# Reordering a fused retention and ELU-MLP kernel: an earlier k^T v' visit, a later first ELU, split input differences, another order of the last seven products

## The chip, the cores and the metric

The kernel runs on one core of a Trainium2 chip. The time is device time in microseconds (us), the median of several executions. Its engines are TensorE (PE for the matmuls, PEld for the loads of their weights), VectorE (DVE), ScalarE (ACT), GpSimd (POOL) and SyncE (SP), which issues the DMA transfers. Every engine works through its own instructions in program order and waits for the others by semaphores.

## The reference

A retention layer (batch 4, 8 heads, sequence 768, head width 64) is followed by a two-layer network with ELU on 3072 tokens, all in fp32:

```python
for t in range(S):
    state = gamma * state + k[:, :, t] (outer) v[:, :, t]
    y[:, :, t] = scale * q[:, :, t] @ state
x = y reshaped to (3072, 512)
h = x @ w_in                                  # (3072, 2048)
g = where(h > 0, h, exp(min(h, 0)) - 1)
out = g @ w_out                               # (3072, 512)
```

## The kernel before

The 3072 tokens go in six blocks (`tb` 0 to 5) of 512. Blocks 2 to 5 use Strassen's scheme (Winograd's form: seven products M1 to M7 instead of eight) once for the first layer in four "quadruples" `n` of the hidden units, and twice for parts of it and for the second layer. The second layer of a block is seven outer products `j`, taken in the order 1, 2, 6, 7, 5, 3, 4, and each of them is again seven small products `k` ("a seven"): four matmuls of 128 columns each. The small products accumulate in PSUM banks pa, pb, pd; M6 and M5 are added onto M1's bank pa, M3 onto the same bank after M5, and M4 onto M7's bank pd. Before a product is added onto a bank, what the bank holds must have been read.

The retention layer of the next block is spread over the present block as short visits: `scores` (step 0), `states` (step 1, the k^T v' products and the running sums of the state), and `outputs` (steps 2 to 4).

The ELU of a tile is two ScalarE passes (relu and exp) and a last VectorE operation, which is put off in a list `later`:

```python
def elu(g, h, depth=1, then=None):
    r = epool.tile([P, 512], FP32, name="r", tag="r", bufs=3)
    ...
    nc.scalar.activation(e, h, AF.Relu, scale=-1.0)       # L390
    nc.scalar.activation(e, e, AF.Exp, scale=-1.0)        # L391
    def last():
        nc.vector.scalar_tensor_tensor(g, e, -1.0, h, ALU.add, ALU.max)   # L394
        if then: then()
    while len(later) >= depth:
        later.pop(0)()
    later.append(last)
```

First layer of a block, and where the second begins (`sec`):

```python
def first_end(n, name, ps, x=None):
    g = gq[name][:, 2 * n : 2 * n + 2, :]
    nc.vector.tensor_tensor(out=g, in0=ps, in1=g if x is None else x, op=ALU.add)   # L748
    ...
    return lambda: elu(g, g, 3, combine if name == "C22" else None)   # combine: T3, T1 (L753)
...
for n in range(NQ):
    rest(n, 6)                       # M6 on TensorE
    u2[n] = kept(qa[n])              # copy out of PSUM on ScalarE
    if n == 0:
        for _ in tail: pass
    if end: end()
    pop()                            # one operation from `later`
    rest(n, 7)                       # M7
    m7 = kept(qd[n])
    pop(2)
    if n == 3:
        next(sec)                    # first two input differences of the second layer
    rest(n, 5)                       # M5
    end = first_end(n, "C12", qa[n])
    other = first_end(n, "C22", qa[n], m7)
    end()
    if n < 3:
        other()
        rest(n + 1, 1)               # M1 of the next quadruple
        first_end(n + 1, "C11", qa[n + 1])()
        rest(n, 4)                   # M4
        end = first_end(n, "C21", qd[n], u2[n])
        pop()
        if n == 0: bring(3)
        elif more: retention_step(tb + 1, n - 1)      # scores behind n = 1, states behind n = 2
for _ in range(2):
    next(sec)                        # two more differences; M1 and M2 of the first seven
other()
rest(3, 4)
end = first_end(3, "C21", qd[3], u2[3])
next(sec)                            # M6, M7 of the first seven
end()
flush()
for step, s in enumerate(sec):
    if step in (1, 3, 5):
        retention_step(tb + 1, 2 + step // 2)
    if s == ORDER2[-1]: break
tail = sec
```

One seven of the second layer, and the loop over the seven of them. `input_parts` makes the four differences of an input (L656), each on a tile of 128 x 512:

```python
def input_parts(j):
    ...
    for n, _ in enumerate(quarters_of_input(t, b11, b12, b21, b22)):   # 4 subtractions, L656
        if n == 1:
            yield                    # after the first two
    ts[j] = {1: b11, 2: b21, 3: b22, 4: t[:, 3], 5: t[:, 0], 6: t[:, 1], 7: t[:, 2]}

def inner(j):
    res = pool.tile([P, 2, 2, P], FP32, name="res", tag=tag)
    pa = bank("a")[:, 0, 0:P]
    product(j, 1, pa, True)          # L779
    m1 = copy(pa)                    # L787, ScalarE
    pb = bank("b")[:, 0, 0:P]
    product(j, 2, pb, True)
    add(res[:, 0, 0], pb, m1)        # L791, VectorE
    yield
    product(j, 6, pa, False)
    u2 = copy(pa)
    pd = bank("d")[:, 0, 0:P]
    product(j, 7, pd, True)
    yield
    product(j, 5, pa, False)
    add(res[:, 1, 1], pd, copy(pa))  # the seven's C22 sum
    yield
    product(j, 3, pa, False)
    nc.scalar.copy(res[:, 0, 1], pa) # L812
    yield
    product(j, 4, pd, False)
    add(res[:, 1, 0], pd, u2)
    sum_up(j, res.rearrange("p d t c -> p (d t c)"))   # adds of 128 x 512, stores (L820)
...
for at, j in enumerate(ORDER2):      # 1, 2, 6, 7, 5, 3, 4
    cur = inner(j)
    next(cur)                        # M1, M2
    if j == 1: yield "tail"
    for _ in before: pass            # M3, M4 and sum_up of the seven before
    if j == 2: flush(); next_input(2)     # four adds, L558
    if j == 5: next_input(6)              # four subtractions, L558
    if j == 1:
        next(cur)
        yield "elu"
        next(cur)
    if at + 1 < 7:
        inputs(ORDER2[at + 1])       # all four differences of the next input
    else:
        behind_last()
    if j != 1:
        next(cur)                    # M6, M7
        next(cur)                    # M5, C22's sum
    before = cur
    yield j
```

`sum_up(4)` adds the outer result of j = 7 and others (`kept2[7]`) to all four quarters at once and stores 256 KB. The weights of the small products are fetched one by one from DRAM into a ring of eleven tiles, in the order of their use (`to_fetch`).

Of the kernel before, what the change touches and what calls it, by code (L numbers as in the profile page):

```python
# [9 lines left out]
FP32 = mybir.dt.float32  # L10
# [7 lines left out]
def kernel(  # L18
# [32 lines left out]
    nc = tc.nc  # L51
# [414 lines left out]
    def bank(x):  # L466
        return ps_f.tile([P, 2, TH], FP32, name="p" + x, tag=x, bufs=2 if x == "a" else 1)
# [140 lines left out]
    for tb in range(2, NTB):  # L608
        for j in TWICE:
            m1, m2, *mine = [(tb, 0, j, k) for k in (1, 2, 6, 7, 5, 4, 3)]  # L610
            to_fetch += [m1] + before[:1] + [m2] + mine[:2] + before[1:] + mine[2:3]
            before = mine[3:]
        to_fetch, before = to_fetch + before, []
        for j in ORDER2:
            mine = [(tb, 1, j, k) for k in (1, 2, 6, 7, 5, 3, 4)]
            to_fetch += mine[:2] + before + mine[2:5]
            before = mine[5:]
        to_fetch, before = to_fetch + before, []
# [140 lines left out]
    def second_twice(tb, behind_last):  # L759
        quarter = lambda x, r, t: x[:, 4 * r : 4 * r + 4, P * t : P * t + P]  # L760
        ts, kept2 = {}, {}

        def inputs(j):
            for _ in input_parts(j):
                pass

        def input_parts(j):
            x, t = gq[INPUT2[j]], tpool.tile([P, 4, 4, P], FP32, name="ts", tag="ts")
            b11, b12, b21, b22 = (quarter(x, a, b) for a in range(2) for b in range(2))
            for n, _ in enumerate(quarters_of_input(t, b11, b12, b21, b22)):  # L770
# [4 lines that stand above are left out]
        def product(j, k, ps, begin):  # L775
            name, w = small_w.pop(0)
            assert name == (tb, 1, j, k)
            for f in range(4):
                nc.tensor.matmul(  # L779
                    ps, lhsT=w[:, f, :], rhs=ts[j][k][:, f, :], start=(begin and f == 0), stop=(f == 3),  # L780
                    skip_group_check=True,
                )
            fetch_small()

        def copy(ps):
            m = small.tile([P, P], FP32, name="ms", tag="ms")
            nc.scalar.copy(m, ps)  # L787
            return m

        def add(o, x, y):  # L790
            nc.vector.tensor_tensor(out=o, in0=x, in1=y, op=ALU.add)  # L791

        def inner(j):
            pool, tag = (mpool, "m") if j in (1, 6, 7, 5) else (hpool, "h")
# [3 lines that stand above are left out]
            m1 = copy(pa)  # L798
            pb = bank("b")[:, 0, 0:P]
            product(j, 2, pb, True)  # L800
            add(res[:, 0, 0], pb, m1)
# [7 lines that stand above are left out]
            add(res[:, 1, 1], pd, copy(pa))  # L809
# [5 lines that stand above are left out]
            add(res[:, 1, 0], pd, u2)  # L815
            sum_up(j, res.rearrange("p d t c -> p (d t c)"))

        def store(name, h):
            r, t = int(name[1]) - 1, int(name[2]) - 1
            nc.sync.dma_start(out[tb, r, t].rearrange("p d c -> p (d c)"), h)  # L820

        def sum_up(j, m):

            kept2[j] = m
            if j == 2:
                add(m, kept2[1], m)
                store("C11", m)
            elif j == 6:
                add(m, kept2[1], m)
            elif j == 5:  # L830
                add(m, kept2[6], m)
                h = hpool.tile([P, 512], FP32, name="h", tag="h")
                add(h, m, kept2[7])
                store("C22", h)
                add(kept2[7], kept2[6], kept2[7])
            elif j == 3:
                add(m, kept2[5], m)
                store("C12", m)
            elif j == 4:
                add(m, kept2[7], m)  # L840
                store("C21", m)

        for _ in input_parts(1):
            yield "input"
        yield "inputs"
        before = iter(())
        for at, j in enumerate(ORDER2):
            cur = inner(j)
            next(cur)
            if j == 1:  # L850
                yield "tail"
            for _ in before:
                pass
            if j == 2:
                flush()
                next_input(2)
            if j == 5:
                next_input(6)
            if j == 1:

                next(cur)
                yield "elu"
                next(cur)
            if at + 1 < 7:
                inputs(ORDER2[at + 1])
            else:
                behind_last()
            if j != 1:
                next(cur)
                next(cur)  # L870
            before = cur
            yield j
        for _ in before:
            yield "rest"
# [121 lines left out]
    for tb in range(2, NTB):  # L996
        more = tb + 1 < NTB
        qa, qd, u2, end = {}, {}, {}, None

        def rest(n, j):  # L1000
            if j == 1:
                qa[n] = ps_r.tile([P, 2, TH], FP32, name="qa", tag="r") if n == 0 else bank("a")
            if j == 7:
                qd[n] = ps_r.tile([P, 2, TH], FP32, name="qd", tag="r") if n == 3 else bank("bd"[n % 2])
            first_rest(n, j, qa[n] if j in (1, 6, 5) else qd[n])

        def bring(n):
            if more:
                load((tb + 1) * CPB + n)
                scale_v((tb + 1) * CPB + n)  # L1010

        def pop(count=1):
            for _ in range(count):
                if later:
                    later.pop(0)()

        bring(0)
        rest(0, 1)
        for _ in tail:
            pass  # L1020
        tail, parts = iter(()), combine_x_parts()
        for at, j in enumerate(TWICE):
            cur = first_twice(tb, j)

            next(cur)
            next(tail, None)
            next(parts, None)
            next(cur)
            for _ in tail:
                pass  # L1030
            next(parts, None)
            if at == 1:

                first_end(0, "C11", qa[0])()
                bring(1)
            next(cur)
            tail = cur
        next(tail)
        bring(2)

        sec = second_twice(tb, combine_x_twice if more else lambda: None)
        for n in range(NQ):

            rest(n, 6)
            u2[n] = kept(qa[n])
            if n == 0:
                for _ in tail:
                    pass
            if end:
                end()  # L1050
            pop()
            rest(n, 7)
            m7 = kept(qd[n])
            pop(2)
            if n == 3:
                next(sec)
            rest(n, 5)
            end = first_end(n, "C12", qa[n])
            other = first_end(n, "C22", qa[n], m7)
            end()  # L1060
            if n < 3:
                other()
                rest(n + 1, 1)
                first_end(n + 1, "C11", qa[n + 1])()
                rest(n, 4)
                end = first_end(n, "C21", qd[n], u2[n])
                pop()
                if n == 0:
                    bring(3)
                elif more:  # L1070
                    retention_step(tb + 1, n - 1)
        for _ in range(2):
            next(sec)
        other()
        rest(3, 4)
        end = first_end(3, "C21", qd[3], u2[3])
        next(sec)
# [6 lines that stand above are left out]
            if s == ORDER2[-1]:  # L1084
                break
        tail = sec
# [49 lines left out]
```

## Time and profile before

| | |
|---|---|
| time, median of 3 runs | 656.89 us (655.04 to 657.96) |
| span of the profiled execution | 655.2 us |
| granted TensorE clock, mean | 0.997 |
| busy, 500 to 550 us (second layer of block 4): PE, PEld, DVE, ACT | 49.28, 47.09, 40.05, 11.86 us |
| DMA | 134.16 MB, mean 205 GB/s |

A row of the timeline gives the start in us, the busy time in us, engine, line and operation, the tile written and the tiles read, the number of instructions merged into the row, and in brackets the idle time of the engine before it with what ended it. A matmul product of four weights is shown as eight records; records overlap, so the busy time of a row is longer than the distance to the next row of a full stream. Line 779 is a small product of the second layer, line 740 a product of the first layer, line 787 a copy out of PSUM, line 791 an add of the second layer, line 656 an input difference. The second layers begin at about 303, 405, 506 and 603 us in blocks 2, 3, 4 and 5.

### The profile page before, as it was taken

Reading aid. Unit: us, or ns where it says so; the run is one execution under the profiler, and the core shown is the slowest. Engines: PE = TensorE matmul, PEld = TensorE weight load, DVE = VectorE, ACT = ScalarE, POOL = GpSimd, SP = SyncE. Lnnn points to the kernel's source line nnn. Section 1 sums busy time; section 2 is a strip of 40 time slices with the busy share of each in tenths; the row PEclk is TensorE's granted clock in tenths of the full one; section 3 lists DMA queues with packets and bytes.
Section 4 is the critical chain, followed back from the end, with each engine's and each line's share of the span. In section 5 each row is a group of like instructions: output and inputs, shape, how many; then the busy total and the mean of one; then the engine's idle time right before and its main releaser. Section 6 shows DMA issues by size and latency. Waiting matters only on the chain.

```text
span 655.2 us, 15245 instructions
## 1 busy us (share of the span) xinstructions
PE 635.3 (97%) x6336; PEld 539.4 (82%) x6336; DVE 470.1 (72%) x825; ACT 237.6 (36%) x448; POOL 37.0 (6%) x36
## 2 busy tenths in 40 slices
PE   4899999999999999999999999999999999999997
PEld 4754444548888889988999988999988999988996
DVE  5688778658866736588867488867488958558964
ACT  7467641104441001555111465211454311366211
POOL 1000100000720000110000110000020000000000
PEclk9899999999999999999999999999999999999999
DMA  8648978446384766911788811788830688700793
GB/s 340 240 134 311 316 232 260 131 126 227 107 298 174 256 231 207 377 76 52 250 276 285 303 77 34 221 277 272 305 135 2 204 270 279 214 18 10 237 313 116
DMA packets 68724, 134.16 MB, mean 205 GB/s; under 512 B 5680, under 2 KB 23088, under 8 KB 66352
## 3 DMA queue, kind: packets, MB, share of 16 engines
q1 hardware_dynamic: 68656, 133.19, 60.9%
q8 instruction: 50, 0.82, 0.5%
q14 instruction: 18, 0.15, 0.1%
HBM read 109.05 MB, written 24.12 MB: 203 GB/s over the span
## 4 chain that ended last, share of the span: by engine, by line
PE 84%; DVE 12%; DMA 2%; issue 1%; SPq 0%; ACT 0%; DVEq 0%
PE pa L779 11%; PE pa L740 8%; PE pd L779 7%; PE hp L420 6%; PE pa L434 4%; PE pa L579 4%; PE pb L740 4%; PE pa L521 4%; PE pa L694 4%; DVE ts L656 3%; PE qa L740 3%; PE pb L779 3%; PE pd L579 2%; DVE gC L394 2%; PE pd L740 2%; PE pd L521 2%
## 5 line engine op out<-in xcount | busy, mean ns | idle before, releaser
L391 ACT ACTIVATE r<-r 128x512 f32<-128x512 f32 x96 | 60.5, 630 | 3.1
L787 ACT COPY ms<-pa 128x128 f32<-128x128 f32 x84 | 22.2, 265 | 107.0 <-PE pa L779 106.8
L779 PE MATMUL pd<-ts,wq 128*128 128x128 f32 x448 | 59.8, 276 | 1.1 <-DVE res L791 1.1
L779 PE MATMUL pa<-ts,wq 128*128 128x128 f32 x448 | 59.4, 275 | 1.3 <-ACT ms L787 1.3
L779 PEld LDWEIGHTS pa<-ts,wq 128*128 128x128 f32 x448 | 54.6, 192 | 2.3 <-ACT ms L787 2.1
L779 PEld LDWEIGHTS pd<-ts,wq 128*128 128x128 f32 x448 | 54.5, 192 | 2.2 <-DVE res L791 2.2
L390 ACT ACTIVATE r<-gC 128x512 f32<-128x512 f32 x64 | 40.0, 625 | 41.1 <-DVE gC L748 41.1
L779 PE MATMUL pa<-gC,wq 128*128 128x128 f32 x384 | 51.7, 278 | 0.4 <-ACT ms L787 0.4
L779 PEld LDWEIGHTS pa<-gC,wq 128*128 128x128 f32 x384 | 47.2, 192 | 1.5 <-ACT ms L787 0.5
L394 DVE SCALAR_TENSOR_TENSOR gC<-r,gC 128x512 f32<-128x512 f32 x64 | 46.7, 757 | 0.7 <-ACT r L391 0.7
L242 POOL TENSOR_TENSOR kvn<-kvn,vf 128x512 f32<-128x512 f32 x20 | 22.9, 1150 | 361.4 <-DMA kvn<-in_qkv_dram 201.6
L791 DVE TENSOR_TENSOR res<-pd,ms 128x128 f32<-128x128 f32 x56 | 16.1, 287 | 35.0 <-PE pd L779 32.6
L471 ACT COPY m<-pa 128x512 f32<-128x512 f32 x27 | 15.7, 581 | 66.1 <-PE pa L579 35.5
L656 DVE TENSOR_TENSOR ts<-gC,ts 128x512 f32<-128x512 f32 x48 | 33.0, 688 | 0.8
L656 DVE TENSOR_TENSOR ts<-gC 128x512 f32<-128x512 f32 x48 | 32.8, 684 | 0.0
L434 PE MATMUL pa<-gC,w_s 128*128 128x512 f32 x64 | 30.6, 600 | 0.0
L579 PE MATMUL pa<-gC,ws 128*128 128x256 f32 x128 | 28.6, 381 | 0.0
L579 PEld LDWEIGHTS pa<-gC,ws 128*128 128x128 f32 x128 | 24.1, 190 | 3.4
L779 PE MATMUL pb<-gC,wq 128*128 128x128 f32 x192 | 26.4, 277 | 0.3
L779 PEld LDWEIGHTS pb<-gC,wq 128*128 128x128 f32 x192 | 23.7, 192 | 1.0 <-DVE gC L394 1.0
L812 ACT COPY res<-pa 128x128 f32<-128x128 f32 x28 | 7.4, 265 | 46.1 <-PE pa L779 44.6
L748 DVE TENSOR_TENSOR gC<-qa,gC 128x512 f32<-128x512 f32 x8 | 5.5, 692 | 25.0 <-PE qa L740 18.3
(192 smaller groups left out, 1290.5 us busy)
## 6 DMA issues: line engine op xcount, KB each, us to landing
wq<-scratch_dram SPq DMA_DIRECT2D x228, 256.0 KB, 4.3
wraw<-in_w_dram SPq DMA_DIRECT2D x16, 1024.0 KB, 6.0
qk<-in_qkv_dram SPq DMA_DIRECT2D x24, 512.0 KB, 7.7
kvn<-in_qkv_dram SPq DMA_DIRECT2D x24, 512.0 KB, 8.2
scratch_dram<-so SPq DMA_DIRECT2D x22, 512.0 KB, 3.2
ws<-scratch_dram SPq DMA_DIRECT2D x7, 1024.0 KB, 8.0
scratch_dram<-w_s SPq DMA_DIRECT2D x8, 512.0 KB, 7.3
out_dram<-res SPq DMA_DIRECT2D x12, 256.0 KB, 4.6
```

What stands on the lines that cost most here:

```text
L242: eng.tensor_tensor(out=kv[:, 1], in0=kv[:, 1], in1=vf[:, i].unsqueeze(2).to_broadcast([C, H, D]), op=ALU.mult)
L390: nc.scalar.activation(e, h, AF.Relu, scale=-1.0)
L391: nc.scalar.activation(e, e, AF.Exp, scale=-1.0)
L394: nc.vector.scalar_tensor_tensor(g, e, -1.0, h, ALU.add, ALU.max)
L420: nc.tensor.matmul(hp, lhsT=w[n][:, fi, j // 2, j % 2, :], rhs=xb[:, j, :], start=(j == 0), stop=(j == 3))
L434: nc.tensor.matmul(ops[d], lhsT=wo[:, row, d * P : (d + 1) * P], rhs=g_plain[row * NF + f], start=(f == 0 and row == 0), stop=(f == NF - 1 ...
L521: nc.tensor.matmul(ps[:, fi, :], lhsT=w[:, fi, j2, :], rhs=x[:, j2, :], start=(begin and fi == 0 and j2 == 0), stop=(j2 == 1), skip_group_ ...
L579: nc.tensor.matmul(ps[:, d, :], lhsT=ws[:, 2 * d + f // 4, f % 4, :], rhs=gq[INPUT2[j]][:, f, :], start=(begin and f == 0 and d == 0), sto ...
L656: sub = lambda o, x, y: nc.vector.tensor_tensor(out=o, in0=x, in1=y, op=ALU.subtract)
L694: nc.tensor.matmul(ps[:, f, :], lhsT=lhs[f], rhs=xs[j][k], start=(begin and f == 0), stop=True, skip_group_check=True,)
L740: nc.tensor.matmul(ps[:, fi, :], lhsT=w[:, fi, j2, :], rhs=x[:, j2, :], start=(j in (1, 7) and fi == 0 and j2 == 0), stop=(j2 == 1), skip_ ...
L779: nc.tensor.matmul(ps, lhsT=w[:, f, :], rhs=ts[j][k][:, f, :], start=(begin and f == 0), stop=(f == 3), skip_group_check=True,)
```

## The change

Five moves, all of order:

1. In blocks 2 to 4 the `states` visit for the next block, which stood behind the third quadruple, now stands inside it, behind M7.
2. In the fourth quadruple of blocks 2 to 5, the ELU passes of C12 are issued behind M1 and M2 of the first seven instead of ahead of them; so the copy of M1 stands ahead of them in ScalarE's order.
3. During j = 2 and j = 5 of every block's second layer, only two of the next input's four differences are issued at the old place, the other two behind the seven's C22 sum.
4. In the last block the last seven (j = 4) takes M4 ahead of M3, on a bank of its own (pb), and the fetch order follows.
5. The last seven adds earlier results to each quarter by itself (where possible before the product) and stores its result in three transfers for four quarters of 64 KB: 64, 128 and 64 KB, instead of one of 256 KB.

It is for keeping TensorE from waiting at the start of the second layer, for reading bank pd in time, and for shortening what follows the last product.

```diff
@@ fetch order of the second layer
+            last = (4, 3) if j == 4 and tb == NTB - 1 else (3, 4)
+            mine = [(tb, 1, j, k) for k in (1, 2, 6, 7, 5) + last]
-            mine = [(tb, 1, j, k) for k in (1, 2, 6, 7, 5, 3, 4)]
@@ the last seven
+        def inner_end(j):
+            res = hpool.tile([P, 2, 2, P], FP32, name="res", tag="h")
+            to = out[tb, 1, 0].rearrange("p d (t c) -> p d t c", t=2)
+            k = kept2[7].rearrange("p (d t c) -> p d t c", d=2, t=2)
...         (M1, M2, M6 as in inner)
+            product(j, 7, pd, True)
+            m7 = copy(pd)
+            yield
+            add(u2, u2, k[:, 1, 0])
+            add(u2, pd, u2)
+            product(j, 5, pa, False)
+            add(res[:, 1, 1], pa, m7)
+            yield
+            add(res[:, 0, 0], res[:, 0, 0], k[:, 0, 0])
+            nc.sync.dma_start(to[:, 0, 0], res[:, 0, 0])
+            add(res[:, 1, 1], res[:, 1, 1], k[:, 1, 1])
+            pb = bank("b")[:, 0, 0:P]
+            product(j, 4, pb, True)
+            add(res[:, 1, 0], pb, u2)
+            nc.sync.dma_start(to[:, 1], res[:, 1])
+            product(j, 3, pa, False)
+            add(res[:, 0, 1], pa, k[:, 0, 1])
+            nc.sync.dma_start(to[:, 0, 1], res[:, 0, 1])
@@ loop over the sevens
-            cur = inner(j)
+            last = j == 4 and tb == NTB - 1
+            cur = (inner_end if last else inner)(j)
...
-            if at + 1 < 7:
-                inputs(ORDER2[at + 1])
+            parts = input_parts(ORDER2[at + 1]) if at + 1 < 7 else iter(())
+            if j in (2, 5):
+                next(parts)
             else:
+                for _ in parts:
+                    pass
+            if at == 6:
                 behind_last()
             if j != 1:
                 next(cur)
                 next(cur)
+            for _ in parts:
+                pass
@@ first layer
             pop(2)
+            if n == 2 and more:
+                retention_step(tb + 1, 1)
             if n == 3:
                 next(sec)
...
-            end()
             if n < 3:
+                end()
                 other()
...
-                elif more:
-                    retention_step(tb + 1, n - 1)
+                elif n == 1 and more:
+                    retention_step(tb + 1, 0)
         for _ in range(2):
             next(sec)
+        end()
         other()
```

More of the change, by code (lines that the diff above doesn't have):

```diff
@@ L816, in inner @@
             sum_up(j, res.rearrange("p d t c -> p (d t c)"))
+        def inner_end(j):
+            res = hpool.tile([P, 2, 2, P], FP32, name="res", tag="h")
+            to = out[tb, 1, 0].rearrange("p d (t c) -> p d t c", t=2)
+            k = kept2[7].rearrange("p (d t c) -> p d t c", d=2, t=2)
+            pa = bank("a")[:, 0, 0:P]
+            product(j, 1, pa, True)
+            m1 = copy(pa)
+            pb = bank("b")[:, 0, 0:P]
+            product(j, 2, pb, True)
+            add(res[:, 0, 0], pb, m1)
+            yield
+            product(j, 6, pa, False)
+            u2 = copy(pa)
+            pd = bank("d")[:, 0, 0:P]
+            product(j, 7, pd, True)
[5 more added lines that the diff above has]
+            add(res[:, 1, 1], pa, m7)
+            yield
+            add(res[:, 0, 0], res[:, 0, 0], k[:, 0, 0])
+            nc.sync.dma_start(to[:, 0, 0], res[:, 0, 0])
+            add(res[:, 1, 1], res[:, 1, 1], k[:, 1, 1])
+            pb = bank("b")[:, 0, 0:P]
+            product(j, 4, pb, True)
[4 more added lines that the diff above has]
+            nc.sync.dma_start(to[:, 0, 1], res[:, 0, 1])
         def store(name, h):
```

## The prediction

> **What bounds the kernel now.** I read the first part of the page, then the starts of all TensorE matmuls in order, then the timeline around each place where a start came late, and last the end of the program.
>
> ```profile
> span 655.2 us, 15245 instructions
> PE 635.3 (97%) x6336; PEld 539.4 (82%) x6336; DVE 470.1 (72%) x825; ACT 237.6 (36%) x448; POOL 37.0 (6%) x36
> ```
>
> TensorE sets the time. The change takes no matmul away, so it can only win idle TensorE time and time after the last matmul. The busy share hides short holes, because a matmul's shown duration overlaps the next one's start. I therefore measure from start to start. A product of four weights on 128 columns (line 779) takes 0.89 us to the next start, one on 256 columns (line 740) takes 1.73 us. What a product starts later than that is lost, and each restart after a wait costs 0.10 more (the first product after one takes 0.99).
>
> First kind of hole, timeline of block 2, where the second stage begins:
>
> ```profile
> 304.69 1.89 PE L740 MATMUL qd<-xt,w_b 128*128 128x256 f32 x8
> 305.94 0.63 ACT L390 ACTIVATE r<-gC 128x512 f32<-128x512 f32 x1 [3.96 <-DVE gC L748]
> 306.60 0.63 ACT L391 ACTIVATE r<-r 128x512 f32<-128x512 f32 x1
> 307.13 0.25 ACT L787 COPY ms<-pa 128x128 f32<-128x128 f32 x1
> 307.44 1.16 PE L779 MATMUL pa<-ts,wq 128*128 128x128 f32 x8 [0.85 <-ACT ms L787]
> ```
>
> M6 of the first seven could start at 304.69 + 1.73 = 306.42 and starts at 307.44. It adds onto bank pa, which must first be copied out. M1, whose sum the copy takes, started at 302.91 and was over at about 304.0, but the copy stands on ScalarE behind the two ELU passes of C12, and these wait for VectorE's C12 sum, done only at 305.9. VectorE is late because the k^T v' visit's adds stand just ahead. Loss 1.02 + 0.10 = 1.12 us. By the same sum, block 4 loses 0.63 + 0.10 = 0.73 (M6 at 509.94 for 509.31); blocks 3 and 5 lose nothing (408.44 and 606.54 are on time).
>
> Second kind, timeline of block 5, second seven (j = 2):
>
> ```profile
> 616.14 0.68 DVE L656 TENSOR_TENSOR ts<-gC 128x512 f32<-128x512 f32 x1
> 616.85 0.69 DVE L656 TENSOR_TENSOR ts<-gC,ts 128x512 f32<-128x512 f32 x1
> 617.54 1.06 PE L779 MATMUL pa<-gC,wq 128*128 128x128 f32 x8
> 618.07 0.69 DVE L656 TENSOR_TENSOR ts<-gC,ts 128x512 f32<-128x512 f32 x1
> 618.67 0.28 DVE L791 TENSOR_TENSOR res<-pd,ms 128x128 f32<-128x128 f32 x1
> 619.01 1.16 PE L779 MATMUL pd<-ts,wq 128*128 128x128 f32 x8 [0.41 <-DVE res L791]
> ```
>
> M4 adds onto pd, so C22's sum must have read pd. That sum had its operands at 616.2 (the copy of M5 ran from 615.96), but stands behind all four differences of the next input. Wanted 618.43, started 619.01: 0.58 + 0.10 = 0.68. The same hole is there for j = 5 in every block: 0.43, 0.43, 0.42 in blocks 2 to 4 (M4 at 342.10, 442.97, 544.62) and 0.43 in block 5 (638.19 for 637.87). For j = 3 in block 5 it is 0.17 + 0.10.
>
> Third, the end:
>
> ```profile
> 647.50 1.06 PE L779 MATMUL pa<-ts,wq 128*128 128x128 f32 x8
> 648.59 0.27 ACT L787 COPY ms<-pa 128x128 f32<-128x128 f32 x1 [1.52 <-PE pa L779]
> 648.91 1.16 PE L779 MATMUL pa<-gC,wq 128*128 128x128 f32 x8 [0.35 <-ACT ms L787]
> 649.91 1.06 PE L779 MATMUL pd<-ts,wq 128*128 128x128 f32 x8
> 651.00 0.29 DVE L791 TENSOR_TENSOR res<-pd,ms 128x128 f32<-128x128 f32 x1 [1.82 <-PE pd L779]
> 651.40 0.69 DVE L791 TENSOR_TENSOR res<-res 128x512 f32<-128x512 f32 x1
> ```
>
> M3 directly after M5 must wait for M5's copy (648.91 for 648.39: 0.52 + 0.10), and behind the last product come a small sum, a sum over all four quarters and a store of 256 KB, issued at 652.12, landed at 654.14, then 1.0 us of closing.
>
> **What the Trainium skill says.** "Perfetto Trace Analysis", Identifying the Most-Contended Engine, calls matmul busy time a poor measure of headroom and weight-load busy time a better one. Here they are 97% and 82%; the starts show why neither is enough, the holes being fractions of a microsecond. "VectorE: DVE Perf Modes", The TRN2 errata, gives an fp32 two-operand sum as (N+151)/0.96 ns: 691 ns at 512 and, worked out, 291 at 128. The trace agrees with 692 and 287 ns; so four quarter sums cost more in all than one large, and only the last one matters. "DMA: Bandwidth & Descriptors", Anatomy of one DMA, puts about 2.0 us of fixed cost on a transfer, most of it the write receipt. Here the whole 256 KB store took 2.02 us from issue to landing, data included: about 0.65 to the first packet, 1.0 of packets, 0.35 to the landing. The trace decides: about 1.0 us is fixed here, and the packets can be shortened.
>
> **The change, part by part.**
>
> *Visit earlier and C12's ELU behind the first copy (blocks 2 to 4; the second also 5).* No instruction is added. The visit (128 or 112 matmuls of 64 columns, then some seven VectorE adds of 424 ns) keeps its price on TensorE: it interrupts the stream once in either place. On VectorE in block 4 the adds run from 499.82 to 503.14, 3.3 us. In the quadruple before it VectorE idles 0.46 + 0.44 + 1.04 = 1.94 us waiting for products (block 2: 0.46 + 0.44 + 1.03). Put there, the adds use that idle time. My walk through the queue of block 4 delays the sums of the third quadruple by some 0.7 us and gets VectorE to the first input difference at about 505.3 instead of 506.40. The copy of M1, now ahead of the ELU, runs when M1 is done, at about 304.0 in block 2, 2.4 us before M6 wants it. Its other operand, the second difference (done at 305.3), is in time as well. So both holes close: **1.12 + 0.73 = 1.85 us**. Blocks 2 to 4 then look like block 5, which has no visit.
>
> A hole stays: M2 of the second seven waits for the last ELU of C21: 0.35, 0.32, 0.36 and 0.28 us in blocks 2 to 5, restart included. Block 5 has it without any visit, so I expect about 0.28 in each: **0.2 us** at most, counted as 0.1.
>
> *Half inputs.* Two of the four differences move behind C22's sum, which comes about 1.25 us earlier (two steps of 0.61 to 0.65). It must gain 0.58 at most, so the holes at j = 2 (block 5) and j = 5 (all) close: 0.68 + 0.43 + 0.43 + 0.42 + 0.43 = **2.39 us**. What moves back is wanted late: the third difference feeds M7 of the next seven, five products (4.5 us) after M5, the fourth M4. For j = 3 nothing changes and 0.27 stays.
>
> *The end.* With M4 (on its own bank pb) between M5 and M3, M4 starts at 648.39 and M3 at 649.28; C22's sum reads pa at 648.6 to 648.9, in time. **0.62 us**. The sums with earlier results move ahead of the last product: u2 takes its addend before M4 is over, two others are done meanwhile. Behind M3 stands one sum of 0.29 us, then its store: M3 ends at about 650.35, store issued at 650.70. Before, the end of M4 (650.97) to the issue took 1.15 us, now 0.35: **0.80 us**. The last store has 64 KB in 512-byte rows; such packets took 27 ns in this trace, the present ones of 2048 bytes 84 ns. Eight per engine: 8 x 57 ns = **0.46 us**. The other parts are issued 0.9 us and more ahead and should be written by then.
>
> Sum: 1.85 + 0.1 + 2.39 + 0.62 + 0.80 + 0.46 = 6.2 us, or 656.89 - 6.2 = 650.7. As one of five terms may come short I say 650.9.
>
> **Rivals.** *A new hole in the third quadruple.* The delayed C12 and C22 sums push three ELUs (ScalarE, 1.19 us each in a row) towards the copy of M6 of the fourth, for which M5 waits. In my walk that copy ends some 0.4 to 0.6 us before M5 wants it in blocks 2 and 4. Against it: the slack is positive. For it: it is small, and if the delay is one microsecond larger, each of three blocks loses up to 0.5. Then 652.2. *VectorE as the bound in the second stage.* It is 80% busy there (40.1 of 50 us from 500 to 550), and in block 5 runs without a break from 607.35 to 618.95. If each hole only moves to the next product that waits for VectorE, half of the 2.39 us is lost: 652. Against it: behind every C22 sum concerned VectorE had over 1 us of idle time waiting for products (1.05 before 620.20). *Weights arriving late.* A faster stream asks for its weights earlier, but the fetches run eleven tiles ahead (9.8 us of products) and land in 4.3 us; in blocks 2 to 5 no hole but one, at 258, waits for one. *The stores at the end in each other's way*: three issues of 0.34 us and an unfinished 128 KB ahead of the last 64 KB could take back 0.4 us.
>
> **Range and chances.** The gain can hardly exceed 7 us, as the holes touched sum to 4.9 and the end to 1.3; if two rivals come true it is 3.5. The times before spread over 2.9 us, so the median itself is uncertain by about one. From 649.0 to 653.5 covers both. Two per cent is 13.1 us, twice all that can be won; a loss of that size would need a new wait of several microseconds in every block. Faster 0.01, same 0.98, slower 0.01.
>
> **What would show it.** In the changed trace M6 of the first seven follows the qd product by 1.73 us in every block; M4 of j = 2 and j = 5 follows M3 by 0.89; the 0.27 at j = 3 and about 0.3 at M2 of the second seven stay; the last product has M3's form (pa), and the span's end comes some 3.0 us after it instead of 4.2. I'm wrong if M5 of the fourth quadruple waits for ScalarE, if M7 of j = 6 or 3 waits for VectorE, or if the span stays above 652.

## The result and the profile after

The changed kernel takes 651.8 us (median of 6 runs, 650.24 to 653.29) against 657.35 us for the kernel before in the same series: a ratio of 0.9918, 95% interval 0.9893 to 0.9943. Three later series gave 0.9898 (0.9868 to 0.9928), 0.9911 (0.9891 to 0.9931) and 0.9912 (0.9897 to 0.9927). That is a gain of 0.8 to 1.0 per cent, clear of the scatter in all four series and below two per cent. The prediction was 650.9 us.

Busy times from the page of the changed kernel, and its chain of work that ended last by engine:

```profile
PE 633.5 (97%) x6336; PEld 539.2 (83%) x6336; DVE 468.8 (72%) x829; ACT 237.7 (37%) x447; POOL 36.8 (6%) x36
...
PE 96%; DMA 1%; DVE 1%; issue 1%; SPq 0%; DVEq 0%
```

The same chain in the kernel before:

```profile
PE 84%; DVE 12%; DMA 2%; issue 1%; SPq 0%; ACT 0%; DVEq 0%
```

Busy shares have hardly moved. What moved is the chain: before, 84% of it lay on TensorE and 12% on VectorE; now 96% and 1%. The 12% is the work on VectorE through which the chain ran, not time lost: the whole gain is about 1%. What is left of waits for VectorE in blocks 2 to 5 is 0.28 us at M2 of each second seven and 0.27 at j = 3 in block 5, restarts included. Code lines are shifted by one and more against the kernel before (779 is now 780, 787 is 788, 791 is 792). The timelines show only the rows that the argument needs.

Timeline of block 2, where the second layer begins:

```profile
304.95 0.27 ACT L788 COPY ms<-pa 128x128 f32<-128x128 f32 x1 [2.03 <-PE pa L780]
305.39 0.63 ACT L390 ACTIVATE r<-gC 128x512 f32<-128x512 f32 x1 [0.17 <-DVE gC L749]
305.65 1.89 PE L741 MATMUL qd<-xt,w_b 128*128 128x256 f32 x8
307.38 1.05 PE L780 MATMUL pa<-ts,wq 128*128 128x128 f32 x8
```

M1's copy is made as soon as M1 is over, and M6 starts 1.73 us after the qd product: no loss (1.02 before).

Timeline of block 5, second seven (j = 2):

```profile
615.76 0.69 DVE L657 TENSOR_TENSOR ts<-gC,ts 128x512 f32<-128x512 f32 x1
616.37 0.28 DVE L792 TENSOR_TENSOR res<-pd,ms 128x128 f32<-128x128 f32 x1
616.45 1.06 PE L780 MATMUL pa<-gC,wq 128*128 128x128 f32 x8
616.57 0.68 DVE L657 TENSOR_TENSOR ts<-gC 128x512 f32<-128x512 f32 x1
617.34 1.06 PE L780 MATMUL pd<-ts,wq 128*128 128x128 f32 x8
```

C22's sum stands behind two differences instead of four, and M4 starts 0.89 us after M3.

Timeline of the end; the stores are on the SP queue:

```profile
645.30 1.06 PE L780 MATMUL pa<-ts,wq 128*128 128x128 f32 x8
646.19 1.06 PE L780 MATMUL pb<-ts,wq 128*128 128x128 f32 x8
647.09 1.06 PE L780 MATMUL pa<-gC,wq 128*128 128x128 f32 x8
647.29 0.29 DVE L792 TENSOR_TENSOR res<-pb,ms 128x128 f32<-128x128 f32 x1 [0.20 <-PE pb L780]
648.18 0.29 DVE L792 TENSOR_TENSOR res<-pa,res 128x128 f32<-128x128 f32 x1 [0.60 <-PE pa L780]
648.50 0.33 SPq L851 DMA_DIRECT2D out_dram<-res  x1
```

M5, M4 and M3 follow each other at 0.89 us. From the last product's end (648.14) to the store's issue are 0.36 us (1.15 before), from issue to landing 1.55 (2.02 before).

One hole is new. In this profile TensorE stands still in block 2, in the middle of a product:

```profile
332.51 0.82 PE L780 MATMUL pa<-gC,wq 128*128 128x128 f32 x5
...
334.33 0.60 PE L780 MATMUL pa<-gC,wq 128*128 128x128 f32 x3 [1.00 <-issue]
```

The sixth record was due at 333.16 and starts at 334.33: 1.17 us, and 0.10 of restart, with no instruction to wait for. It is followed up below.

A single span depends on this and on the first 45 us, so I compare the distances between the starts of successive blocks' first products, in us. Block 2 also has up to 0.5 us of waiting for weights at its start, different in each profile. A star marks profiles with the standstill (its size in brackets).

| kernel | block 2 | block 3 | block 4 | block 5 to end |
|---|---|---|---|---|
| before | 100.70 | 100.87 | 101.66 | 99.38 |
| changed, first profile | 99.90* (1.27) | 100.40 | 100.42 | 96.35 |
| changed, second profile | 99.06 | 100.41 | 100.42 | 96.35 |
| visit alone | 101.21* (1.82) | 100.82 | 100.84 | 99.35 |
| copy ahead of ELU alone | 101.17* (0.80) | 100.85 | 101.64 | 99.36 |
| half inputs alone | 99.81 | 100.44 | 101.22 | 98.26 |
| last seven alone | 100.60 | 100.86 | 101.64 | 97.44 |
| order of the last seven alone | 102.04* (1.54) | 100.87 | 101.66 | 98.59 |
| changed, copy behind ELU again | 98.84 | 100.41 | 100.42 | 96.35 |
| changed, two differences later | 99.49 | 100.86 | 100.87 | 96.53 |
| changed, one difference on GpSimd | 99.54 | 100.60 | 100.62 | 96.27 |
| changed, finer order | 98.34 | 100.12 | 100.13 | 95.80 |

### The profile page after: what moved, and what is told of

Same layout as the page of the kernel before. It is cut to its first block, busy times and chain, and to the rows that moved or that the text cites. A ratio compares the mean times of both kernels' runs of the same rounds, so it can differ in the third digit from the quotient of the medians.

```text
span 651.1 us, 15255 instructions
## 1 busy us (share of the span) xinstructions
PE 633.5 (97%) x6336; PEld 539.2 (83%) x6336; DVE 468.8 (72%) x829; ACT 237.7 (37%) x447; POOL 36.8 (6%) x36
## 4 chain that ended last, share of the span: by engine, by line
PE 96%; DMA 1%; DVE 1%; issue 1%; SPq 0%; DVEq 0%
PE pa L780 16%; PE pa L741 10%; PE pd L780 8%; PE hp L420 6%; PE pa L695 4%; PE pa L434 4%; PE pa L579 4%; PE pb L741 4%; PE pa L521 4%; PE pb L780 4%; PE qa L741 3%; PE pd L695 2%; PE pd L579 2%; PE qd L741 2%; PE pd L521 2%; PE pd L741 2%
## 5 line engine op out<-in xcount | busy, mean ns | idle before, releaser
L780 PE MATMUL pd<-ts,wq 128*128 128x128 f32 x440 | 58.2, 275 | 0.0
L394 DVE SCALAR_TENSOR_TENSOR gC<-r,gC 128x512 f32<-128x512 f32 x64 | 44.5, 727 | 0.7 <-ACT r L391 0.7
```

Of the source, the lines that this page charges most:

```text
L780: nc.tensor.matmul(ps, lhsT=w[:, f, :], rhs=ts[j][k][:, f, :], start=(begin and f == 0), stop=(f == 3), skip_group_check=True,)
```

## The experiments

**The four parts, one at a time.** Each is the kernel before with one part of the change.

*The visit alone:*

```diff
             pop(2)
+            if n == 2 and more:
+                retention_step(tb + 1, 1)
...
-                elif more:
-                    retention_step(tb + 1, n - 1)
+                elif n == 1 and more:
+                    retention_step(tb + 1, 0)
```

> The kernel before with the states visit alone moved behind M7 of the third quadruple. My theory: VectorE reaches C12's sum of the fourth quadruple about 1.1 us earlier, so the copy of M1, still behind C12's ELU passes, ends before M6 wants it; M6 of the first seven is on time in blocks 2 and 4: 1.12 + 0.73 = 1.85 us and about 0.1 at M2 of the second seven, block 2 shorter by 1.2, block 3 by 0.05, block 4 by 0.8, block 5 unchanged. Rival one: the copy must also get ahead of the ELU, then at least 0.3 us stays at M6 in block 2. Rival two: the visit's adds delay C12 and C22 of the third quadruple so that M5 of the fourth waits for ScalarE, 0.3 to 0.5 us in each of blocks 2 to 4.

Measured: ratio 0.9966 (0.9956 to 0.9976), 2.2 us. Block 2 without the standstill 99.4, block 4 shorter by 0.82, block 3 by 0.05, as my theory had it. In the kernel before, where M1 starts at 302.91, VectorE's first input difference of block 2 is this row:

```profile
303.89 0.69 DVE L656 TENSOR_TENSOR ts<-gC 128x512 f32<-128x512 f32 x1
```

Timeline of block 2 with the visit moved; the second row is M1:

```profile
303.92 0.68 DVE L656 TENSOR_TENSOR ts<-gC 128x512 f32<-128x512 f32 x1
304.44 1.05 PE L779 MATMUL pa<-gC,wq 128*128 128x128 f32 x8
...
305.97 0.63 ACT L390 ACTIVATE r<-gC 128x512 f32<-128x512 f32 x1 [2.47 <-DVE gC L748]
...
307.17 0.25 ACT L787 COPY ms<-pa 128x128 f32<-128x128 f32 x1
...
307.95 1.05 PE L779 MATMUL pa<-ts,wq 128*128 128x128 f32 x8
```

VectorE's date shows the cause. In the kernel before, its first input difference starts 0.98 us after M1 in block 2 and 0.60 after it in block 4, but 0.17 ahead in block 3 and 0.51 ahead in block 5, which has no visit. With the visit moved, it starts 0.51 to 0.52 us ahead of M1 in all four blocks. The copy still stands behind an ELU, but the ELU now starts early enough: copy over at 307.42, M6 at 307.95, 1.73 after the qd product (306.23). No wait at M5 of the fourth quadruple (rival two) is to be seen.

*The copy ahead of the ELU alone:*

```diff
-            end()
             if n < 3:
+                end()
                 other()
...
         for _ in range(2):
             next(sec)
+        end()
         other()
```

> The kernel before with C12's ELU passes of the fourth quadruple alone issued behind M1 and M2 of the first seven. My theory: M6 is on time everywhere (gain 1.85 us), but VectorE is as late as before, so C12's and C22's ELU passes end late and the copy of M6 behind them ends late: a new hole at M5 of the first seven, about 0.6 us in block 2 and 0.1 to 0.2 in block 4. Net gain about 1.0 us. Rival: this move alone closes everything, 1.85 us, and the visit's move brings nothing.

Measured: ratio 1.0002 (0.9990 to 1.0014), nothing. The rival fell, and of my theory only the hole at M5 came true (0.40 us for 0.6); the net gain did not. Timeline of block 2:

```profile
308.27 0.25 ACT L787 COPY ms<-pa 128x128 f32<-128x128 f32 x1
...
308.57 1.16 PE L779 MATMUL pa<-ts,wq 128*128 128x128 f32 x8 [0.24 <-ACT ms L787]
...
311.02 0.68 DVE L394 SCALAR_TENSOR_TENSOR gC<-r,gC 128x512 f32<-128x512 f32 x1
...
311.76 0.71 PE L779 MATMUL pb<-gC,wq 128*128 128x128 f32 x4 [0.69 <-DVE gC L394]
```

M6 is on time, but M5 now waits 0.40 and M2 of the second seven 0.86 (0.25 before), plus 0.10 each. Its input is C21's last ELU operation, which ends 7.05 us after the start of the qd product here (311.70 and 304.65) and 7.06 us after it in the kernel before (311.75 and 304.69): in both kernels VectorE works from 303.9 to that date without a break, so its queue alone sets it. The hole of 1.12 merely moved to the next products that depend on VectorE; in block 4 nearly all of it moved to M2 (0.85, 0.26 before).

*The half inputs alone:*

```diff
-            if at + 1 < 7:
-                inputs(ORDER2[at + 1])
+            parts = input_parts(ORDER2[at + 1]) if at + 1 < 7 else iter(())
+            if j in (2, 5):
+                next(parts)
...
+            for _ in parts:
+                pass
```

> The kernel before with the half inputs alone (j = 2 and j = 5). My theory: M4 of j = 2 in block 5 and of j = 5 in blocks 2 to 5 start 0.89 us after M3: gain 2.39 us, 0.43 in each of blocks 2 to 4 and 1.11 in block 5; the 0.27 at j = 3 in block 5 stays. Rival: VectorE is the bound there and half of it comes back at the next product that waits for it (M7 of j = 6 or j = 3, or M4 of j = 6): gain 1.2 us.

Measured: ratio 0.9958 (0.9946 to 0.9970), 2.8 us. Blocks 3 and 4 shorter by 0.43 and 0.44, block 5 by 1.12; the 0.27 at j = 3 stays. No hole comes back; the rival fell.

*The last seven alone* (`inner_end` and its fetch order), and *its order alone*, with one sum and one store as before:

```diff
+            m7 = copy(pd)
...
+            add(u2, pd, u2)
             product(j, 5, pa, False)
+            add(res[:, 1, 1], pa, m7)
...
+            pb = bank("b")[:, 0, 0:P]
+            product(j, 4, pb, True)
+            add(res[:, 1, 0], pb, u2)
             product(j, 3, pa, False)
             nc.scalar.copy(res[:, 0, 1], pa)
             sum_up(j, res.rearrange("p d t c -> p (d t c)"))
```

> The kernel before with the last seven alone changed (M4 ahead of M3, sums by quarters, three stores). My theory: block 5 to the end shorter by 0.62 + 0.80 + 0.46 = 1.9 us, blocks 2 to 4 unchanged. Rival: the three stores get in each other's way or the write receipt is all that counts: then the 0.46 is missing and the gain is 1.4 us or less.

> The kernel before with M4 ahead of M3 on its own bank in the last seven, but the sum over four quarters behind it and one store of 256 KB as before. My theory: only the 0.62 us at M3 is won, block 5 to the end 98.8 instead of 99.4 us, and the end comes 4.2 us after the last product as before. Rival: the order alone brings the whole 1.9 us.

Measured for all of it: ratio 0.9976 (0.9966 to 0.9987), 1.6 us, block 5 to the end 97.44, 1.94 us less. For the order alone, in one profiled execution: 98.59 (98.8 expected), 0.79 less: the 0.62 at M3, and 0.10 because a copy of 0.27 us instead of a sum of 0.29 and its gap stands ahead of the large sum, the rest in the closing; from issue to landing 2.01 us as before. In the full version it is 1.55: the size of the last store counts, and not only the part of a store that its size does not change (the rival's "write receipt"). The stores ahead do not disturb it: the first of the three, of 64 KB too and with no store in flight, took 1.54. The four single gains add up to 0.51, 1.30 and 3.11 us in blocks 3, 4 and 5, against 0.46, 1.24 and 3.03 of the whole change, so the parts hardly act on each other.

**Is the copy's move of any use, and is the standstill part of the kernel?** The second of these two is the changed kernel with this part undone.

> The changed kernel once more, to have its gain with a narrower interval beside what follows, and a second profile. From block 2's start to the end it should again be some 5.5 to 6.8 us shorter than the kernel before. In the first profile TensorE stood still for 1.27 us at 333 in block 2 with nothing shown as the cause, as it did in the two experiments with the visit alone and the copy alone, but not in the kernel before. If it belongs to the kernel, it is there again; if it is chance of an execution, it is gone or elsewhere.

> The changed kernel with C12's ELU passes back at their old place, ahead of M1's copy. After the two single experiments my theory is now that the visit's move alone brings the whole gain at the second layer's start and the copy's place brings nothing: the same time as the changed kernel within 0.2 us in the blocks' lengths, M6 on time in all blocks. Rival (the prediction's own): both are needed or the copy's place alone closes M6's hole; then holes at M6 of up to 1.1 us come back in blocks 2 and 4.

Measured in one series: changed 0.9898 (0.9868 to 0.9928), without the copy's move 0.9883 (0.9857 to 0.9910); blocks 3, 4 and 5 equal to 0.01 us. The copy's move brings nothing: once VectorE is early, the copy is early enough in either place. The standstill is absent in both profiles, and in the two later ones of the changed kernel. It was in 4 of the 14 profiles, among them the order of the last seven alone, which changes nothing before block 5. So it is chance of an execution, not part of the change.

**Can the holes that stayed be closed?** First, two differences of the fourth quadruple behind C21's last ELU operation, and halves for j = 3:

```diff
-        return lambda: elu(g, g, 3, combine if name == "C22" else None)
+        if n == 3 and name == "C21":
+            return lambda: elu(g, g, 3, combine)
+        return lambda: elu(g, g, 3, combine if name == "C22" and n < 3 else None)
...
-            if j in (2, 5):
+            if j in (2, 5, 3):
```

> The changed kernel and two moves more: in the fourth quadruple VectorE makes the two differences of C22, C12 and C11 behind C21's last ELU operation instead of ahead of it, and j = 3 has its input differences in halves too. If the hole at M2 of the second seven is VectorE's order (two differences of 0.7 us ahead of the operation waited for), it closes in all four blocks, and so does the 0.27 at M4 of j = 3 in block 5: 4 x 0.28 + 0.27 = 1.4 us less than the changed kernel. Rival, as the copy alone showed it: VectorE as a whole is late there, and the hole only moves on to the next product that waits for it (M4 of j = 1 or M6 of j = 2): no gain but the 0.27.

Measured: ratio 0.9908 (0.9882 to 0.9933), the changed kernel in the same series 0.9898. Both holes are closed, but each block has a new one of 0.59 + 0.10, at M7 of the second seven:

```profile
313.99 0.28 DVE L794 TENSOR_TENSOR res<-pd,ms 128x128 f32<-128x128 f32 x1
...
314.33 1.16 PE L782 MATMUL pd<-ts,wq 128*128 128x128 f32 x8 [0.43 <-DVE res L794]
```

M7 needs pd free, and the sum of j = 1 that reads pd stands behind everything else. Moreover VectorE idled 0.49 us at 308.6, as C21's ELU passes were not yet done. The rival came true in kind, at M7 and not at M4 or M6 where it had the new hole; the blocks are 0.18 to 0.45 us longer than in the changed kernel.

Second, one of the two differences on GpSimd (and halves for j = 3):

```diff
-            sub(mine("T1"), mine("C12"), mine("C11"))
+            nc.gpsimd.tensor_tensor(out=mine("T1"), in0=mine("C12"), in1=mine("C11"), op=ALU.subtract)
```

> The changed kernel, on the same chip as the next, to compare with it: 0.990 of the kernel before, holes of 0.28 at M2 of the second seven in blocks 2 to 5 and of 0.27 at j = 3 in block 5.

> The changed kernel, with the difference C12 - C11 (needed only at j = 5) moved from VectorE to GpSimd in every quadruple of blocks 2 to 5, and with j = 3's input differences in halves. The last version showed that a new order on VectorE alone only moves the hole, because it works there without a break. If its amount of work is the limit, 0.69 us less ahead of C21's last ELU operation closes the hole at M2 and opens none: 4 x 0.28 + 0.27 = 1.4 us less than the changed kernel. Rival: GpSimd, slower and with transfers to wait for in its own order, is late for the sum that overwrites C11 at j = 2, or slows VectorE while both work; then no gain or a loss.

Measured: ratio 0.9910 (0.9892 to 0.9928), the changed kernel beside it 0.9911 (0.9891 to 0.9931): no gain. Timeline of block 2:

```profile
309.10 1.65 POOL L756 TENSOR_TENSOR gC<-gC,gC 128x512 f32<-128x512 f32 x1 [7.26 <-DVE gT L754]
...
309.74 1.56 DVE L657 TENSOR_TENSOR ts<-gC 128x512 f32<-128x512 f32 x1
...
313.69 1.16 PE L780 MATMUL pd<-ts,wq 128*128 128x128 f32 x8 [0.18 <-DVE res L792]
```

While GpSimd works, VectorE's difference takes 1.56 us instead of 0.68: the 0.69 taken off its queue comes back as 0.88. The holes at M2 and at j = 3 are closed, but a new one of 0.34 to 0.39 + 0.10 stands at M7 of the second seven in each block: the rival came true.

Third, a finer order on VectorE alone. C12 - C11 goes behind C21's ELU, C22 - C12 stays ahead of it; of j = 2's input differences the fourth goes behind the sum that frees pd; halves for j = 3:

```diff
             sub(mine("T3"), mine("C22"), mine("C12"))
-            sub(mine("T1"), mine("C12"), mine("C11"))
+            if n < 3:
+                sub(mine("T1"), mine("C12"), mine("C11"))
...         (for n == 3 behind C21's last ELU operation)
-            parts = input_parts(ORDER2[at + 1]) if at + 1 < 7 else iter(())
-            if j in (2, 5):
+            parts = input_parts(ORDER2[at + 1], 2 if j == 1 else 1) if at + 1 < 7 else iter(())
+            if j in (1, 2, 5, 3):
...         (for j == 1 the rest of `parts` behind `before` of the next round)
```

> The changed kernel, on the same chip as the next, to compare with it: 0.990 to 0.991 of the kernel before.

> The changed kernel with a finer order on VectorE, nothing moved to GpSimd: in the fourth quadruple C22 - C12 stays ahead of C21's last ELU operation (it fills the time until ScalarE is done), C12 - C11 goes behind it; of the input differences for j = 2 the fourth goes behind the C21 sum of j = 1; j = 3's are in halves. If only the order of the operations ahead of each wait counts, the holes at M2 of the second seven and at j = 3 close and none opens at M7 of the second seven: 1.4 us less than the changed kernel, blocks 2 to 4 shorter by 0.28 and block 5 by 0.55. Rival: VectorE has no room there, and a hole at M7 or M4 of the second seven stays as in the two versions before it.

Measured: ratio 0.9899 (0.9882 to 0.9916), 650.96 us; the changed kernel beside it 0.9912 (0.9897 to 0.9927), 651.69 us. The intervals overlap; the blocks decide: 0.29, 0.29 and 0.55 us shorter in blocks 3, 4 and 5, exactly the holes. What is left of waits for weight loads in blocks 2 to 5 of its profile:

```profile
PEld sc L268 <- issue: 1.0, 3, 0.3
PEld kv L290 <- issue: 1.0, 3, 0.3
```

Only the entries into the visits remain. This version has the shortest blocks of all.

## Why the prediction was right

- **Second layer's start, 1.85 us.** Right in size: both holes closed. Right in the mechanism for the visit: it was to bring VectorE to block 4's first input difference 1.1 us earlier (505.3 for 506.40), and against M1 that difference moved from 0.60 behind to 0.51 ahead. Wrong in one step: "Its other operand ... is in time as well. So both holes close" credited the copy's move with closing them, together with the visit. The runs showed that the visit does it alone (2.2 us) and the copy's move nothing, alone or on top. The prediction itself had the reason, "VectorE is late": moving the copy leaves VectorE's date for C21 where it was.
- **M2 of the second seven**: "I expect about 0.28 in each": measured 0.18 + 0.10 in all four blocks.
- **Half inputs, 2.39 us.** Blocks 3 and 4 and block 5 gained 0.43, 0.44 and 1.12 in the single experiment; the working gave 0.43, 0.42 and 1.11.
- **The end.** 0.79 for the sums (0.80 predicted), 0.47 for the smaller store (0.46), and M3's wait gone. The prediction's split of the old store was misread: its first packet begins 0.84 us after the issue, not 0.65, the packets span 0.83, not 1.0, so about 1.2 us is fixed here and not 1.0. The 0.46 came from the packets' own times and does not rest on it. With the waits before it, block 5 gained 3.03 us; the predicted terms for it, 0.68 + 0.43 + 0.62 + 0.80 + 0.46, make 2.99.
- **By block.** Blocks 3 and 4 gained 0.46 and 1.24; the terms give 0.43 + 0.04 and 0.73 + 0.42 + 0.08. All blocks of the second profile: 1.64 + 0.46 + 1.24 + 3.03 = 6.4 us, against 6.2.
- **The rivals.** None came true in the change itself. "VectorE as the bound" did in two of the three further versions, where the hole moved to M7; the third, with the same work in a finer order, closed every hole.
- **The medians** show 5.1 to 7.1 us in four series; about 6.2 lies within all four intervals. The rest is scatter between executions, of which the profiles show two sources (below).

## What to carry to other kernels

When an in-order engine runs without a break, moving one of its consumers ahead closes a hole only to open it at the next consumer; what helps is to put its work where it idles, or to put behind each awaited operation what isn't awaited yet. Count waits from start to start, and follow each hole to the next operation with the same supplier before its size is put into the sum. At the end of a kernel, finish everything but the last product's share ahead of it, and make the last store small.

## What the runs showed of the hardware

**Standstills of TensorE's instruction supply.** The trace has packets of 16 KB of a queue of the kind "instruction", some ten microseconds apart in block 2. I take the queue to be TensorE's: it has 50 such packets, and TensorE has 12672 matmuls and weight loads, 253 to a packet. In the four profiles with a standstill, all at the same instruction, the packet before it began at 331.96, 333.03, 331.70 and 333.95 us, and that instruction began 2.35 to 2.43 us later. In the other ten profiles the packet began 2.67 to 5.05 us ahead of it, and nothing stood still. That the fetch takes about 2.4 us and came too late fits all fourteen; no run was made to test it, and why it starts late in some executions stays open. The Trainium skill, "Runtime: NRT & Kernel Launch", Instruction fetch mechanics, describes refills of 16 KB that are mostly hidden; here they are, but for 0.8 to 1.8 us in 4 of 14 profiles.

**GpSimd against VectorE.** In the version with GpSimd's difference, VectorE operations with two SBUF inputs took up to 1.76 us while it ran, but sums with an operand in PSUM stayed at 0.68 to 0.69. "SBUF — State Buffer", SBUF: two separate sides, says that a GpSimd operation and a VectorE operation with two SBUF inputs lock each other out of a shared pair of ports; the trace agrees.

**The start.** TensorE's granted clock was at half near the start for 3.4 us in some profiles, 6.8 us in others and not at all in two. The same long stretch of first-layer matmuls (line 420) began at 40.6 and 40.8 us in the two, at 40.9 to 42.1 with 3.4 us, and at 42.4 to 43.2 with 6.8. That spread of 2.6 us is as much as the largest part of this change brought, and is why the blocks are compared and not the spans.
